# The issuing queue of a fallback path that sits behind a range test: SyncE's hardware queue or GpSimd's software queue

## The chip, the cores and the metric

One core of one Trainium2 chip runs the kernel. The metric is the device time of one execution, in microseconds (us). Engines are named as in the profile: PE (TensorE matmul), PEld (TensorE weight load), DVE (VectorE), ACT (ScalarE), POOL (GpSimd), SP (SyncE). A "q" behind a name (SPq, POOLq) is the engine's sequencer, which issues DMAs, waits on semaphores and branches.

## The reference

Chunked attention feeds a two-layer network with an exact GELU. q, k and v have 8 batches, 8 heads, 576 positions and 64 channels, in f32; a chunk has 64 positions and attends to itself alone.

```
scores = scale * matmul(q_c, k_c.T)          # per chunk of 64
scores = scores - max(scores, axis=-1)
attn   = exp(scores); attn = attn / (sum(attn, axis=-1) + 1e-09)
out    = matmul(attn, v_c)
x = out.transpose(0, 2, 1, 3).reshape(4608, 512)
h = x @ w_in                                  # 512 -> 2048
g = 0.5 * h * (1 + erf(h / sqrt(2)))
return g @ w_out                              # 2048 -> 512, f32
```

## The kernel before, in words

**Fast path.** Everything from line 1093 to line 1331 is written out by hand under a manual schedule, in nine tiles `t` of 512 tokens. Tiles 0 to 7 are the first 512 positions of each batch; tile 8 is the last chunk of all eight batches. For each tile q, k and v are loaded in f32 by SP, cast to bf16 (mostly on POOL), transposed, multiplied, and exponentiated on ACT without taking off the row's maximum. The sums' reciprocals go on DVE. Both matrix products of the network run on PE in 128 x 128 blocks, in tiles from 1 on with seven block products in place of eight (`seven_rows`, `mm2_seven`, lines 598 and 758), GELU on ACT. The results go to DRAM from SP, and in the last tile partly from ACT (`store_block`, line 870; `last_piece`, line 977, whose copy out of PSUM is line 974).

**Range test.** The fast path has not subtracted the maximum, so all its sums of exponentials are kept. `range_test` (line 875) finds per partition whether all lie between 2^-40 and 2^40; `range_count` (line 887) adds the 128 verdicts with a matmul of one column (line 890), and DVE casts the count to an integer (line 891). Then each of the five engines loads that integer into a register (line 1332) and branches on it (line 1333):

```
range_count()
in_range = nc.values_load(total)
with tc.If(in_range < P, preferred_fallthrough_block=False):
    general()
```

With these inputs all 128 partitions are in range, so `general()` isn't entered.

**General path.** `general` (line 893) loads both weights again and casts them, and then runs `one_chunk` (line 910) in two hardware loops over batches and chunks: three loads, attention with the maximum taken off, the network, one store. Its DMAs are issued by SP: lines 899, 904, 915 and 970.

**What the program does at such an If.** Each DMA of the kernel adds 16 to one of eight semaphores of its queue when it has landed, and each engine adds to its own semaphore. So that the counts agree behind the If whichever way it went, the block for the branch not taken into `general` adds what the body would have added once. The profile has this block's instructions under line 1333. Both ways meet in a last block, under line 1358: SP waits for the DMA semaphores, the five sequencers' and the engines' semaphores, then a barrier over five engines, collected and released by POOL, then POOL clears the range of semaphores that was used, then a second barrier. A first barrier of this kind, also collected by POOL, stands at the start, under line 1347, behind a few register moves and four memsets of constants.

Of the kernel before, what the change touches and what calls it, by code (L numbers as in the profile page):

```python
# [11 lines left out]
def kernel(  # L12
# [9 lines left out]
    nc = tc.nc  # L22
# [5 lines left out]
    B, H, S, D = q.shape  # L28
    CH = 64
# [71 lines left out]
    w_in_v = moe_w_in.rearrange("(ks p) n -> p ks n", p=P)  # L101
    w_out_v = moe_w_out.rearrange("(f p) n -> p f n", p=P)
# [15 lines left out]
    def stage_tile():  # L118
        return stage.tile([P, SW], f32, tag="stage", name="arrival")
# [773 lines left out]
    def general():  # L893

        SUBS = mybir.AluOpType.subtract
        for c in range(4):
            n = d_ff // 4
            raw = stage_tile()[:].rearrange("p (ks n) -> p ks n", ks=KS)
            nc.sync.dma_start(raw, w_in_v[:, :, c * n:(c + 1) * n])
            DV(w_in_sb[:, :, c * n:(c + 1) * n], raw)  # L900
        for c in range(4):
            n = FF // 4
            raw = stage_tile()[:].rearrange("p (f n) -> p f n", f=n)
            nc.sync.dma_start(raw, w_out_v[:, c * n:(c + 1) * n, :])
            DV(w_out_sb[:, c * n:(c + 1) * n, :], raw)
        with tc.For_i(0, B, 1) as b:
            with tc.For_i(0, S, CH) as s0:
                one_chunk(b, s0, SUBS)

    def one_chunk(b, s0, SUBS):  # L910
        rows = bass.ds(s0, CH)
        nat = {}
        for nm, src in (("q", q), ("k", k), ("v", v)):
            raw = stage_tile()[0:CH, 0:d_model]
            nc.sync.dma_start(raw.rearrange("p (h d) -> p h d", h=H),
                              src[bass.ds(b, 1), :, rows, :].rearrange("o h key d -> key (o h) d"))
            nat[nm] = ld.tile([P, G, J, 2, D], bf16, tag="k", name=nm + "_rows", bufs=3)[:].rearrange(
                "p g j r d -> p (g j r d)")[0:CH, 0:d_model]
            DV(nat[nm], raw)
        turned = {}  # L920
        for nm in "qk":
            tp = ps_tp.tile([P, G, CH], bf16, tag="tp", name="tp")
            for g in range(G):
                nc.tensor.transpose(tp[:, g], nat[nm][:, P * g:P * (g + 1)], ident[0:CH, 0:CH])
            turned[nm] = work.tile([P, CT, CH], bf16, tag="pT", name=nm + "_t", bufs=5)[:, 0:G]
            DV(turned[nm], tp[:])
        s_ps = [ps_at.tile([P, G, CH], f32, tag="at", name="s_ps") for _ in range(2)]
        top = work.tile([P, 2, 2, NB], f32, tag="total", name="top", bufs=2)[:].rearrange("p a b c -> p (a b c)")
        less = stage_tile()[0:CH, 0:d_model].rearrange("p (g r c) -> p g r c", g=G, r=2)
        for r in range(2):  # L930
            sl = slice(CH * r, CH * (r + 1))
            for g in range(G):
                nc.tensor.matmul(s_ps[r][0:CH, g], turned["q"][sl, g], turned["k"][sl, g], start=True, stop=True)
            m = top[0:CH, G * r:G * (r + 1)]
            nc.vector.tensor_reduce(m, s_ps[r][0:CH], axis=mybir.AxisListType.X, op=mybir.AluOpType.max)
            nc.vector.tensor_tensor(less[:, :, r], s_ps[r][0:CH], m.to_broadcast([CH, G, CH]), op=SUBS)
        less = less.rearrange("p g r c -> p (g r) c")
        e = stage_tile()[0:CH, 0:d_model].rearrange("p (h c) -> p h c", h=H)
        nc.scalar.activation(e, less, Act.Exp, scale=scale)
        nc.vector.tensor_reduce(top[0:CH, H:2 * H], e, axis=mybir.AxisListType.X, op=ADD)  # L940
        nc.vector.tensor_scalar(top[0:CH, H:2 * H], top[0:CH, H:2 * H], 1e-9, None, op0=ADD)
        nc.vector.reciprocal(top[0:CH, 2 * H:3 * H], top[0:CH, H:2 * H])
        a = work.tile([P, CT, CH], bf16, tag="pT", name="a", bufs=5)[0:CH]
        nc.vector.tensor_tensor(a, e, top[0:CH, 2 * H:3 * H].to_broadcast([CH, H, CH]), op=mybir.AluOpType.mult)
        tp = ps_tp.tile([P, H, CH], bf16, tag="tp", name="tp")
        for h in range(H):
            nc.tensor.transpose(tp[0:CH, h], a[:, h], ident[0:CH, 0:CH])
        aT = work.tile([P, CT, CH], bf16, tag="pT", name="a_t", bufs=5)[0:CH]
        DV(aT, tp[0:CH])
        av = ps_at.tile([P, G, CH], f32, tag="at", name="av")  # L950
        for h in range(H):
            sl = slice(CH * (h % 2), CH * (h % 2 + 1))
            nc.tensor.matmul(av[sl, h // 2], nat["v"][:, D * h:D * (h + 1)], aT[:, h], start=True, stop=True)
        x = work.tile([P, CT, CH], bf16, tag="pT", name="x", bufs=5)[:, 0:G]
        DV(x, av[:])
        hb = hpool.tile([P, FF, MT], bf16, tag="h", name="h")[:, :, 0:CH]
        for a0 in range(0, FF, 8):
            h_ps = ps_mm.tile([P, 8, CH], f32, tag="mm", name="h_ps")
            for f in range(8):
                for ks in range(KS):  # L960
                    nc.tensor.matmul(h_ps[:, f], w_in_sb[:, ks, (a0 + f) * P:(a0 + f + 1) * P], x[:, ks],
                                     start=(ks == 0), stop=(ks == KS - 1))
            nc.scalar.activation(hb[:, a0:a0 + 8], h_ps[:], Act.Gelu)
        y_ps = ps_mm.tile([P, d_model], f32, tag="mm", name="y_ps")
        for f in range(FF):
            nc.tensor.matmul(y_ps[0:CH], hb[:, f], w_out_sb[:, f, :], start=(f == 0), stop=(f == FF - 1))
        y_sb = ypool.tile([P, d_model], f32, tag="y", name="y_sb")
        DV(y_sb[0:CH], y_ps[0:CH])
        by_batch = out.rearrange("(b s) d -> b s d", s=S)
        nc.sync.dma_start(by_batch[bass.ds(b, 1), rows].rearrange("o key d -> (o key) d"), y_sb[0:CH])  # L970

    def last_piece(t, m, y_ps):
        y_sb = ypool.tile([P, HD], f32, tag="y", name="y_sb")
# [119 lines left out]
    with tc.manual_schedule():  # L1093
# [62 lines left out]
        for c in range(1, NWC):  # L1156
# [8 lines left out]
            if c < 3:  # L1165
                r = slice(CH * (c - 1), CH * c)
                o = slice(CH * (2 - c), CH * (3 - c))
# [84 lines left out]
        for t in range(1, NT):  # L1252
            n = t + 1
# [79 lines left out]
        with tc.If(in_range < P, preferred_fallthrough_block=False):  # L1333
            general()
# [28 lines left out]
```

## Time and profile before

| what | value |
|---|---|
| median of 3 runs | 267.47 us |
| lowest and highest of them | 267.15 and 268.73 us |
| the profiled execution | 269.52 us |
| its span, first to last instruction | 267.7 us |
| mean granted TensorE clock | 0.993 |
| instructions in the span | 7854 |
| moved by DMA | 54.02 MB, 123415 packets |

The profile is of one execution. Its own time is 269.52 us, 1.8 us more than the span between its first and last instruction, and 2.05 us more than the median of the three runs without a profile. A row of a line's instructions gives the engine, the operation, how many there were, the least, median and greatest duration in ns, and the start of the first and the last in us from the span's start. A row of the timeline has start and duration in us, and in square brackets the idle time before it and what ended it.

### The profile page before, as it was taken

The page shows a single profiled execution, that of the slowest core. Times are in us where ns is not written, and L with a number is a line of the kernel's source. Part 1 is how long each engine was busy: PE and PEld are TensorE (multiplying, and loading weights), DVE is VectorE, ACT ScalarE, POOL GpSimd, SP SyncE. Part 2 cuts the span into 40 slices and gives each one's busy share as a digit, 9 for nine tenths or more (in the row PEclk, how much of TensorE's full clock was granted, in tenths as well). Part 3 has the DMA queues.
Part 4 walks back from the last instruction along what each step waited for, and adds up shares of the span by engine and source line. Part 5 has one row for each costly group of instructions (what it writes and reads, how often), then busy time and mean ns, then how long its engine had stood idle before and what let it go on. Part 6 is the DMA issues. An engine that isn't in the chain of part 4 may idle for free.

```text
span 267.7 us, 7854 instructions
## 1 busy us (share of the span) xinstructions
PE 256.5 (96%) x3116; PEld 211.7 (79%) x3122; DVE 223.3 (83%) x397; ACT 190.4 (71%) x386; POOL 104.7 (39%) x229
## 2 busy tenths in 40 slices
PE   6599999999999999999999999999999999999992
PEld 2378865556888888887888888898888888888881
DVE  5767786998997687678999999999999999848771
ACT  3666667987767978898887588947894788237610
POOL 7778578702375370570390094087211300000000
PEclk9979999999999999999999999999999999999999
DMA  6999998979889999989999998999963310130014
GB/s 198 259 327 399 393 402 213 288 192 284 238 223 247 185 254 254 231 221 249 279 243 207 284 211 219 184 173 210 275 150 86 123 42 2 40 120 1 2 39 122
DMA packets 123415, 54.02 MB, mean 202 GB/s; under 512 B 97776, under 2 KB 120304, under 8 KB 123376
## 3 DMA queue, kind: packets, MB, share of 16 engines
q1 hardware_dynamic: 123072, 53.23, 78.0%
q8 instruction: 25, 0.41, 0.6%
q10 hardware_dynamic: 304, 0.26, 0.3%
q14 instruction: 14, 0.11, 0.1%
HBM read 36.70 MB, written 9.44 MB: 172 GB/s over the span
## 4 chain that ended last, share of the span: by engine, by line
PE 70%; ACT 8%; SPq 7%; DMA 6%; DVE 3%; POOL 2%; issue 2%; POOLq 0%; ACTq 0%
PE hs_ps L598 23%; PE y_ps L758 18%; PE y_ps L788 9%; PE h_ps L462 5%; ACT h L606 3%; DMA arrival<-in_q_dram 3%; SPq L152 3%; SPq L136 3%; PE y_ps L1021 3%; DMA arrival<-in_k_dram 2%; ACT k_bd L219 2%; PE h_ps L478 2%; PE av_ps L346 1%; DMA out_dram<-kept 1%; PE y_ps L985 1%
## 5 line engine op out<-in xcount | busy, mean ns | idle before, releaser
L606 ACT ACTIVATE h<-hs_ps 128x512 bf16<-128x512 f32 x87 | 49.7, 610 | 6.9 <-PE hs_ps L598 6.0
L235 POOL CAST v_nat<-arrival 128x256 bf16<-128x256 f32 x56 | 25.9, 488 | 37.3 <-DMA arrival<-in_v_dram 36.8
L598 PEld LDWEIGHTS <-w_in_sb 128*128 128x128 bf16 x348 | 33.9, 98 | 4.6 <-issue 0.2
L193 POOL CAST q_nat<-arrival 128x256 bf16<-128x256 f32 x40 | 17.9, 495 | 48.3 <-DMA arrival<-in_q_dram 26.8
L598 PE MATMUL hs_ps<-x,w_in_sb 128*128 128x256 bf16 x232 | 31.7, 272 | 0.0
L758 PEld LDWEIGHTS <-h 128*128 128x128 bf16 x240 | 23.2, 98 | 2.8
L1091 ACT ACT_TABLE_LOAD x16 | 20.5, 1283 | 1.0 <-PEq L1347 0.8
L718 ACT COPY kept<-y_ps 128x512 f32<-128x512 f32 (+1 forms) x17 | 9.0, 535 | 16.0 <-PE y_ps L758 13.0
L189 POOL CAST k_nat<-arrival 128x256 bf16<-128x256 f32 x48 | 18.6, 430 | 3.2 <-DMA arrival<-in_k_dram 3.2
L758 PE MATMUL y_ps<-w_out_sb,h 128*128 128x256 bf16 x160 | 18.6, 273 | 0.0
L758 PE MATMUL y_ps<-v_bd,k_bd 128*128 128x256 bf16 x160 | 18.5, 273 | 0.1
L758 PEld LDWEIGHTS <-k_bd 128*128 128x128 bf16 x160 | 15.6, 98 | 2.1 <-issue 0.2
L615 ACT COPY hs_ps<-hs_ps 128x512 f32<-128x512 f32 x29 | 16.2, 582 | 0.6 <-PE hs_ps L598 0.5
L598 PE MATMUL hs_ps<-k_bd,w_in_sb 128*128 128x256 bf16 x116 | 16.6, 273 | 0.0
L490 ACT ACTIVATE h<-h_ps 128x512 bf16<-128x512 f32 x21 | 12.5, 604 | 5.1 <-PE h_ps L462 3.6
L269 ACT ACTIVATE pT<-s_ps 128x512 bf16<-128x512 f32 x28 | 14.4, 599 | 1.8 <-PE s_ps L261 1.8
L788 PEld LDWEIGHTS <-h 128*128 128x128 bf16 x144 | 13.8, 98 | 1.7
L598 PE MATMUL hs_ps<-k_bd,w_in_more 128*128 128x256 bf16 x96 | 14.2, 273 | 0.0
L462 PE MATMUL h_ps<-x,w_in_sb 128*128 128x256 bf16 x128 | 14.2, 273 | 0.0
L598 PEld LDWEIGHTS <-w_in_more 128*128 128x128 bf16 x128 | 12.5, 98 | 2.0 <-issue 0.3
L723 DVE TENSOR_TENSOR kept<-y_ps,kept 128x512 f32<-128x512 f32 (+1 forms) x16 | 10.4, 651 | 4.0 <-PE y_ps L758 2.3
L462 PEld LDWEIGHTS <-w_in_sb 128*128 128x128 bf16 x128 | 12.4, 98 | 1.6 <-DVE w_in_sb L1066 0.2
(174 smaller groups left out, 640.2 us busy)
## 6 DMA issues: line engine op xcount, KB each, us to landing
arrival<-in_v_dram SPq DMA_DIRECT2D x58, 128.0 KB, 3.2
arrival<-in_k_dram SPq DMA_DIRECT2D x28, 256.0 KB, 5.8
arrival<-in_q_dram SPq DMA_DIRECT2D x7, 1024.0 KB, 6.7
out_dram<-kept SPq DMA_DIRECT2D x24, 256.0 KB, 3.1
arrival<-in_moe_w_out_dram SPq DMA_DIRECT2D x4, 1024.0 KB, 12.4
arrival<-in_moe_w_in_dram SPq DMA_DIRECT2D x6, 512.0 KB, 7.9
out_dram<-y_sb SPq DMA_DIRECT2D x8, 256.0 KB, 3.1
arrival<-in_v_dram SPq DMA_DIRECT2D x28, 64.0 KB, 2.8
```

Of the source, the lines that this page charges most:

```text
L189: copy(st[nm][:, q0:q0 + 2, g], st[nm + "f"][:, 2 * q0:2 * q0 + 4, g].rearrange("p (q r) d -> p q r d", r=2))
L193: copy(st[nm][:, g, j:j + 2].rearrange("p j r d -> p r j d"), st[nm + "f"][:, 2 * g:2 * g + 2, j:j + 2])
L235: copy(st["v"][:, r::2, n], st["vf"][:, r::2, n])
L269: nc.scalar.activation(pT[:].rearrange("p u (c j) -> p u c j", j=J), tiles[t]["s_ps"][m // 2][m % 2][:].rearrange("p u (j c) -> p u c j", ...
L462: nc.tensor.matmul(to[:, cols], left, right[:, cols], start=(start and a == 0), stop=stop, skip_group_check=True)
L490: nc.scalar.activation(tiles[t]["h"][:, f, :], h_ps[:], Act.Gelu)
L598: nc.tensor.matmul(hs[:, f], left[:, ks, f * P:(f + 1) * P], right[:, ks], start=(fresh and f == 0 and ks == 0), stop=(ks == 1), skip_grou ...
L606: nc.scalar.activation(h[:, n:n + HM, HD * c:HD * (c + 1)], src, Act.Gelu)
L615: "s11": lambda: AC(place_of("b")[:], bank["a"][:]),
L758: nc.tensor.matmul(to, left(f, m), right[:, f], start=(fresh and (split or m == 0) and f == 0), stop=(f == HF - 1), skip_group_check=True)
L788: nc.tensor.matmul(bank[name][:, m], left(f, m), right[:, f], start=(fresh and m == 0 and f == 0), stop=(f == HF - 1), skip_group_check=True)
L1091: nc.scalar.activation(act_scratch[:], rest[:, 0:1], func)
```

## The change

All DMAs of the general path are issued by GpSimd (POOL) on its software queue, where they were issued by SP on its hardware queue: four loads of `w_in`, four of `w_out`, and per chunk the loads of q, k and v and the store.

```
@@ general
-            nc.sync.dma_start(raw, w_in_v[:, :, c * n:(c + 1) * n])
+            nc.gpsimd.dma_start(raw, w_in_v[:, :, c * n:(c + 1) * n])
...
-            nc.sync.dma_start(raw, w_out_v[:, c * n:(c + 1) * n, :])
+            nc.gpsimd.dma_start(raw, w_out_v[:, c * n:(c + 1) * n, :])
@@ one_chunk
-            nc.sync.dma_start(raw.rearrange("p (h d) -> p h d", h=H),
+            nc.gpsimd.dma_start(raw.rearrange("p (h d) -> p h d", h=H),
...
-        nc.sync.dma_start(by_batch[bass.ds(b, 1), rows].rearrange("o key d -> (o key) d"), y_sb[0:CH])
+        nc.gpsimd.dma_start(by_batch[bass.ds(b, 1), rows].rearrange("o key d -> (o key) d"), y_sb[0:CH])
```

In the built programs the 7,742 instructions between the first barrier and the branch are the same on every engine, but that ACT once counts two instructions one by one where it added 2 behind the second. Outside `general` these differ:

| place | before | after |
|---|---|---|
| start, line 1347 | SP: 4 register moves ahead of the barrier | POOL: the 4 register moves, behind its INC_SWDGE_SEM and ahead of its memsets |
| not-taken block, line 1333, SP | 8 EVENT_SEMAPHORE, each waits for one of the 8 DMA semaphores of SP's queue and adds to it; branch | branch alone |
| not-taken block, POOL | branch alone | 4 EVENT_SEMAPHORE on the 8 new semaphores of the software queue (waits for 0 or more), one INC_SWDGE_SEM that adds 16 or 32 to each of the 8, branch |
| last block, line 1358, SP | 8 EVENT_SEMAPHORE, the last for ACT's last store | 4 more ahead of these, each waits for two of the new semaphores to have what INC_SWDGE_SEM adds |
| last block, POOL | clears 17 semaphores | clears 25 |
| instructions that the branch to the last block jumps over | SP 91, POOL 44 (ACT 51, DVE 70) | SP 62, POOL 91 (ACT 59, DVE 79) |

INC_SWDGE_SEM is in the program before once, at its start, with no semaphore to add to.

## The prediction

> **What bounds the kernel now.** I read the page first: engine shares, then the chain that ended last.
>
> ```profile
> span 267.7 us, 7854 instructions
> ...
> PE 256.5 (96%) x3116; PEld 211.7 (79%) x3122; DVE 223.3 (83%) x397; ACT 190.4 (71%) x386; POOL 104.7 (39%) x229
> ...
> PE 70%; ACT 8%; SPq 7%; DMA 6%; DVE 3%; POOL 2%; issue 2%; POOLq 0%; ACTq 0%
> ```
>
> PE is busy for 96% of the span and carries 70% of the chain. The diff touches nothing that PE does before the branch, so the question is what lies outside that stretch. The table by windows cuts the span into start, body, last matmuls and tail, and the chain from 250 us on shows where the last compute ends.
>
> ```profile
> 0.00:10.00 10.00, 6.46 (x40) 2.62 (x40) 5.88 (x12) 4.31 (x7) 7.00 (x25) 1.00 0.83 242
> 10.00:239.00 229.00, 226.47 (x2862) 188.19 (x2869) 199.49 (x351) 173.65 (x356) 97.66 (x205) 0.99 0.87 219
> 239.00:262.50 23.50, 23.50 (x217) 20.88 (x214) 17.42 (x33) 12.42 (x25) 0.00 (x0) 1.00 0.13 35
> 262.50:267.70 5.20, 0.10 (x2) 0.01 (x1) 0.48 (x2) 0.00 (x0) 0.00 (x0) 0.96 0.38 107
> ```
> ```profile
> 250.28 12.24 PE y_ps L758 x112
> 262.52 0.02 issue
> 262.54 0.43 DVE y_sb L974
> 262.97 0.05 DVE small L891
> ```
>
> The columns of the windows are busy PE, PEld, DVE, ACT, POOL, then clock, DMA share and GB/s. In the last 5.2 us no engine computes more than 0.48 us: that tail consists of stores landing and of sequencers. There, and at the first barrier, lies all that the change can move. Next I read the instructions of each line of the tail.
>
> ```profile
> L977 SPq DMA_DIRECT2D out_dram<-y_sb x2: 490/492/494, 262.1 to 263.0; - x2
> ...
> DMA to landing us min/median/max: 2.0/2.2/2.4
> ```
> ```profile
> L1332 POOLq TENSOR_LOAD <-small x1: 489/489/489, 263.1 to 263.1; - x1
> ...
> L1332 SPq TENSOR_LOAD <-small x1: 953/953/953, 263.5 to 263.5; - x1
> ```
> ```profile
> L1333 SPq EVENT_SEMAPHORE  x8: 17/17/17, 265.0 to 265.5; - x8
> L1333 POOLq COMPARE_BRANCH  x2: 38/42/45, 263.6 to 263.7; - x2
> ...
> L1333 DVEq COMPARE_BRANCH  x2: 51/53/55, 263.8 to 264.0; - x2
> L1333 SPq COMPARE_BRANCH  x2: 38/48/57, 264.6 to 265.5; - x2
> L1333 ACTq COMPARE_BRANCH  x2: 38/44/49, 264.6 to 264.8; - x2
> ```
> ```profile
> L1358 SPq EVENT_SEMAPHORE  x8: 28/28/28, 266.1 to 266.5; - x8
> L1358 SPq DRAIN  x2: 7/10/13, 266.6 to 266.6; - x2
> L1358 POOLq DRAIN  x1: 41/41/41, 263.8 to 263.8; - x1
> ...
> L1358 DVEq DRAIN  x1: 47/47/47, 264.6 to 264.6; - x1
> L1358 ACTq DRAIN  x1: 8/8/8, 264.9 to 264.9; - x1
> L1358 POOLq EVENT_SEMAPHORE  x1: 17/17/17, 266.7 to 266.7; - x1
> ```
>
> Only SP is late. POOL, DVE and ACT stand at their DRAIN of the last block by 263.8, 264.6 and 264.9; SP reaches its own at 266.6 and POOL's barrier starts at 266.7. SP's way there: the last store is issued at 263.0 (0.49 us), the register is loaded from 263.5 (0.95), the branch comes at 264.6, the first of the eight additions of the not-taken block runs at 265.0 (the store of 263.0, at the least 2.0 us to landing, ends that wait), the eighth at 265.5, so 0.5/7 = 0.07 us each. The second branch at 265.5 reaches the last block at 266.1, and its eight waits take until 266.5: 0.4/7 = 0.06 us each.
>
> **The change, part by part.** `general` isn't entered, so none of its loads and stores is run, and no transfer moves from one queue to another in this execution. What is run and differs is four pieces of sequencer work.
>
> 1. SP's eight additions go. SP then meets its two branches as POOL does now, 0.1 us apart: the second at 264.7 in place of 265.5. The landing that held the first addition until 265.0 is next asked for in the last block.
>
> 2. SP's jump. The rows give two sizes: POOL 263.7 to 263.8 and ACT 264.8 to 264.9, 0.1 us; DVE 264.0 to 264.6 and SP 265.5 to 266.1, 0.6. ACT skips 51 instructions and DVE 70; SP will skip 62, between them, so 0.1 and 0.6 are the ends, and I take 0.5, near SP's own row: it reaches the last block at 265.2 (264.8 to 265.3).
>
> 3. SP's last block has twelve waits in place of eight: 12 x 0.06 = 0.75 us, to 265.95. The hardware queue's landings cannot hold it: SP's and ACT's last stores are issued at 263.0 and land 2.0 to 2.4 us later, at 265.4 at the latest, and the wait for ACT's is the twelfth. Before, this point was 266.55. So pieces 1 to 3 give -0.6 us, with ends of -1.0 and -0.5.
>
> 4. POOL's additions. Four waits that hold at once, and one INC_SWDGE_SEM that adds to eight semaphores. The trace has this operation once, with nothing to add, at the start:
>
> ```profile
> L1347 POOLq EVENT_SEMAPHORE  x2: 17/17/17, 0.6 to 0.6; - x2
> L1347 POOLq INC_SWDGE_SEM  x1: 27/27/27, 0.1 to 0.1; - x1
> L1347 POOL MEMSET const-float32-0.0<- x1: 104/104/104, 0.2 to 0.2; 128x1 f32 x1
> ...
> L1347 POOLq DRAIN  x1: 197/197/197, 0.3 to 0.3; - x1
> ```
> ```profile
> L1347 SPq MOVE  x4: 29/34/42, 0.0 to 0.2; - x4
> L1347 SPq DRAIN  x1: 7/7/7, 0.3 to 0.3; - x1
> ```
> ```profile
> L1358 POOLq EVENT_SEMAPHORE_RANGE_CLEAR  x1: 135/135/135, 267.3 to 267.3; - x1
> ```
>
> POOL branches at 263.7; four waits at no more than 0.1 us each put INC_SWDGE_SEM at 264.1 at the latest. Call its time until all eight semaphores are seen x. SP asks for them from 265.2 on, so x up to 1.1 us costs nothing: the cover is SP's longer register load and its jump, and beyond it every us of x is a us of the end. POOL's own jump now skips 91 instructions as SP's did, 0.6 us, and ends at 264.8 + x, also before 265.95. From the rows x is at the least the 0.03 us of the empty form. Eight additions one after the other at SP's rate are 8 x 0.07 = 0.55; a clear of 17 semaphores in one operation took 0.135. The far end is a landing, 2.4 us, if the additions travel as those of a DMA do. I take 0.5, by the nearest row, SP's additions of the same amounts: hidden.
>
> 5. The clear of 25 semaphores in place of 17 lies on the path: between nothing and 0.135 x 8/17 = +0.06; I take +0.05.
>
> 6. The start. POOL runs four moves that SP ran, ahead of its memsets and its DRAIN; the other engines are at the barrier by 0.3 and POOL collects it at 0.6, so POOL is last and the moves delay all that follows. At 0.034 us of duration they cost 0.14; at SP's pitch (four in 0.3 us) 0.3. I take +0.2. SP's loss of the moves brings nothing, as it waits for POOL.
>
> Sum: -0.6 + 0 + 0.05 + 0.2 = -0.35 us. The profiled execution took 269.52 us, 1.8 more than its span; so 269.15. The median of the runs shown, 267.47, is 2.05 lower, and becomes 267.1.
>
> [...] The page's instruction-fetch queue reads:
>
> ```profile
> q8 instruction: 25, 0.41, 0.6%
> ...
> q14 instruction: 14, 0.11, 0.1%
> ```
>
> By the first row a fetch is 0.6% of 16 engines' 267.7 us over 25 packets, about 1.0 us. [...]
>
> **The rivals.**
>
> A. Slower: the additions land as a DMA's do. x is then 2.0 to 2.4 us, SP sees the semaphores at 266.1 to 266.5 in place of 265.2, and +0.9 to +1.3 comes on top: 268.0 to 268.4. It decides from x = 1.1 + 0.35 = 1.45 us on. For it: these semaphores belong to the software queue, and all that the trace shows of DMA semaphores are landings. Against it: the empty form took 0.03 us, and a memset followed it from 0.2 on.
>
> B. Slower by much: POOL must bring in the code of an operation that it has run only in its empty form. The nearest row of such a load is ACT's:
>
> ```profile
> L1091 ACT ACT_TABLE_LOAD x1 | 1.3, 1283 | 0.8 <-PEq L1347 0.8
> ```
>
> At 1.3 us, beside the 0.5 of the additions, x is 1.8: +0.7 on the sum, 267.8. Two or more such loads in a row reach 269 to 271. [...] The trace has nothing of the kind in the one use it shows.
>
> C. Nothing changes: the not-taken way is not bound by SP's additions, for instance because SP's jump takes as long as it needs for the block to be there, whenever it is asked. SP's last block would then start at 266.0 still (-0.1), four more waits come on top (+0.25), and pieces 5 and 6 add 0.25: +0.4, 267.9 at the most; with half of that loss, 267.7. That the change does nothing at all to the executed instructions is excluded by the list of the two programs.
>
> **How the numbers follow.** The forecast, a small gain of 0.1 to 0.8 us (266.7 to 267.4), has 0.55. Rival A has 0.2, B 0.12 (a third of it within 1%), C 0.13. A per cent is 2.7 us, about what a measurement of this kernel can tell from no change. The range must hold the forecast, A and C, and the spread of the median itself (the three runs before lie from 267.15 to 268.73): 266.3 to 268.7. Beyond 1%: faster 0.01, since all SP's sequencer time between 264.6 and 266.5 is less than 2.7 us; slower 0.08, the far part of B. The rest, 0.91, is within 1%.
>
> **What would show it.** SP's rows under line 1333: two COMPARE_BRANCH about 0.1 us apart and no EVENT_SEMAPHORE; under line 1358 twelve waits, the first about 2.7 us behind the start of the last copy (265.2 less 262.54). A first wait much later, with POOL's INC_SWDGE_SEM long or its semaphores late, is A or B. A first wait at 266 with POOL done by 265 is C. At the start POOL's barrier at 0.75 in place of 0.6. A body that differs, between 10 and 262 us, would make the whole account wrong, as would a longer time outside the span: 1.8 us here, which holds nothing that I can cost.

## The result and the profile after

The kernel after takes 267.37 us (median of 22 runs, 266.05 to 268.92), the kernel before in the same session 268.25 us (22 runs, 267.15 to 270.15). The ratio is 0.9964 with a 95% interval of 0.9948 to 0.998, so the change is worth -0.96 us (-1.4 to -0.5). Ratios here leave out disturbed runs, which the medians beside them contain, so the two need not agree to the last digit.

The forecast was -0.35 us, to 267.1 us. The change is within 1%, a small gain as forecast, and the time lies in the range; but the gain is larger than the sum said, and 0.96 us lies above the 0.1 to 0.8 us of the forecast, though the interval reaches into them. That 267.37 us comes so near to 267.1 is luck: the forecast started from a median of three runs, 267.47 us, which lay 0.78 us below the 268.25 of all 22. The profiled execution of the kernel after took 266.46 us.

First its page and its table by windows, in the columns of the one shown for before: PE, PEld, DVE, ACT, POOL busy, clock, DMA share, GB/s.

```profile
span 264.9 us, 7861 instructions
...
PE 255.6 (97%) x3122; PEld 210.7 (80%) x3122; DVE 223.4 (84%) x397; ACT 190.6 (72%) x386; POOL 106.7 (40%) x229
```
```profile
10.00:239.00 229.00, 227.29 (x2885) 188.72 (x2883) 200.27 (x353) 174.99 (x357) 99.36 (x204) 1.00 0.88 221
239.00:260.60 21.60, 21.60 (x199) 19.17 (x197) 16.56 (x32) 11.19 (x23) 0.00 (x0) 1.00 0.11 26
260.60:264.90 4.30, 0.07 (x1) 0.00 (x0) 0.47 (x2) 0.00 (x0) 0.00 (x0) 0.93 0.46 131
```

The spans differ by 2.8 us, three times what the runs show. Most of that lies ahead of the last copy, in work that is the same in both programs: the copy starts at 262.54 us before and at 260.62 here. In second profiles of the same two kernels it starts at 260.39 and 261.37, the other way about. A single pair of spans cannot show a change of 1 us in this kernel. What repeats is the tail, from the start of the last copy (line 974) to the end: 5.19 and 5.17 us before, 4.30 and 4.29 after. All times "behind the copy" below count from there and are taken from the records in ns; the rows give the same to 0.1 us.

The rows of the not-taken block, of the last block and of the last copy in the kernel after:

```profile
260.62 0.42 DVE L974 COPY y_sb<-y_ps 128x256 f32<-128x256 f32 x1 [0.45 <-PE y_ps L758]
```
```profile
L1333 POOLq EVENT_SEMAPHORE  x4: 17/43/43, 261.9 to 262.1; - x4
L1333 POOLq COMPARE_BRANCH  x2: 38/42/45, 261.8 to 262.4; - x2
...
L1333 SPq COMPARE_BRANCH  x2: 38/50/61, 262.6 to 262.8; - x2
...
L1333 POOLq INC_SWDGE_SEM  x1: 173/173/173, 262.2 to 262.2; - x1
```
```profile
L1358 SPq EVENT_SEMAPHORE  x14: 17/28/28, 263.3 to 264.9; - x14
L1358 POOLq EVENT_SEMAPHORE  x4: 17/17/17, 264.1 to 264.8; - x4
...
L1358 SPq DRAIN  x3: 7/7/13, 264.0 to 264.4; - x3
...
L1358 POOLq EVENT_SEMAPHORE_RANGE_CLEAR  x1: 178/178/178, 264.4 to 264.4; - x1
```

SP has no additions under line 1333, and its two branches stand 0.11 us apart. Its second branch comes 2.14 us behind the copy (before: 3.00), its twelve waits start at 2.65 (before: eight, at 3.51), and it reaches its DRAIN at 3.42 (before: 4.03). That is -0.61 us. POOL's four waits and its INC_SWDGE_SEM of 0.17 us are over by 1.75, long before SP asks for them.

The rest of the tail is POOL's closing barrier. These are its first two semaphore instructions there, in narrow windows of the two traces, before and then after:

```profile
L1358 POOLq EVENT_SEMAPHORE  x2: 17/17/17, 266.7 to 267.0; - x2
```
```profile
L1358 POOLq EVENT_SEMAPHORE  x2: 17/17/17, 264.1 to 264.2; - x2
```

Before, 0.37 us lie between their starts, after 0.09: -0.28 us, at a place where the diff changes nothing. The clear of the semaphores took 0.178 us in place of 0.135 (+0.04), the DRAIN ahead of it 0.09 in place of 0.15. SP's -0.61, the pause's -0.28 and the clear's +0.04 with the DRAIN's -0.06 add up to -0.91, where the tail lost 0.89.

The start did move as forecast, from before to after:

```profile
0.25 0.10 POOL L1347 MEMSET const-float32-0.0<- 128x1 f32 x1 [0.25 <-issue]
...
4.50 0.40 PE L206 MATMUL tp<-ident,q_nat 128*128 128x128 bf16 x4
```
```profile
0.48 0.10 POOL L1347 MEMSET const-float32-0.0<- 128x1 f32 x1 [0.48 <-issue]
...
4.73 0.46 PE L206 MATMUL tp<-ident,q_nat 128*128 128x128 bf16 x4
```

POOL's first memset and the first matmul on data are both 0.23 us later behind the first instruction of the span. Yet the measured time doesn't carry it: time less span is 1.8 us before and 1.58 after (medians over all runs), 0.22 less. The section on the reasons comes back to this.

### The profile page after: what moved, and what is told of

Its sections match the earlier page's. It is cut to its first block, busy times and chain, and to the rows that moved or that the text cites. A ratio compares the mean times of both kernels' runs of the same rounds, so it can differ in the third digit from the quotient of the medians.

```text
span 264.9 us, 7861 instructions
## 1 busy us (share of the span) xinstructions
PE 255.6 (97%) x3122; PEld 210.7 (80%) x3122; DVE 223.4 (84%) x397; ACT 190.6 (72%) x386; POOL 106.7 (40%) x229
## 4 chain that ended last, share of the span: by engine, by line
PE 84%; ACT 8%; DVE 3%; DMA 2%; issue 1%; SPq 1%; POOL 0%; POOLq 0%
PE hs_ps L598 29%; PE y_ps L758 22%; PE y_ps L788 12%; PE h_ps L462 5%; PE y_ps L1021 3%; ACT h L606 3%; PE h_ps L488 2%; DMA arrival<-in_k_dram 2%; ACT k_bd L219 2%; PE av_ps L346 2%; PE h_ps L478 2%; ACT pT L269 2%; PE y_ps L985 1%; PE s_ps L261 1%; PE y_ps L462 1%
## 5 line engine op out<-in xcount | busy, mean ns | idle before, releaser
L189 POOL CAST k_nat<-arrival 128x256 bf16<-128x256 f32 x48 | 20.1, 467 | 2.6 <-DMA arrival<-in_k_dram 2.6
```

The lines of the kernel that those rows point to most:

```text
L189: copy(st[nm][:, q0:q0 + 2, g], st[nm + "f"][:, 2 * q0:2 * q0 + 4, g].rearrange("p (q r) d -> p q r d", r=2))
```

## The experiments

Twelve kernels were run. The table gives what the tail of each shows, in us behind the start of its last copy; "pause" is the time between the starts of POOL's first two semaphore instructions in the closing barrier, "position" the place of POOL's last block in its program, counted in instructions of the built program.

| kernel | SP's second branch | SP's DRAIN | pause | position | tail | tail less 5.19 | ratio to before, 95% interval |
|---|---|---|---|---|---|---|---|
| before, twice | 3.00, 2.98 | 4.03, 4.00 | 0.37, 0.37 | 324 | 5.19, 5.17 | 0 | 1 |
| after, twice | 2.14, 2.13 | 3.42, 3.42 | 0.09, 0.09 | 380 | 4.30, 4.29 | -0.89 | 0.9964 (0.9948 to 0.998) |
| chunk | 2.99 | 4.14 | 0.09 | 361 | 5.02 | -0.17 | 1.0015 (0.9987 to 1.0042) |
| weights | 2.43 | 3.70 | 0.09 | 351 | 4.58 | -0.61 | 0.9955 (0.9918 to 0.9992) |
| act | 2.99 | 4.03 | 0.37 | 324 | 5.19 | 0.00 | 0.9972 (0.994 to 1.0004) |
| empty | 2.14 | 2.96 | 0.08 | 281 | 3.76 | -1.43 | 0.9937 (0.9909 to 0.9965) |
| place | 2.11 | 2.94 | 0.09 | 324 | 3.75 | -1.44 | 0.9964 (0.9932 to 0.9996) |
| pad | 3.00 | 4.03 | 0.08 | 372 | 4.83 | -0.36 | one run |
| page | 2.99 | 4.01 | 0.37 | 452 | 5.17 | -0.02 | one run |
| early9 | 1.10 | 4.21 | 0.09 | 380 | 5.09 | -0.10 | 1.0023 (0.9997 to 1.0049) |
| early9_sp | 4.43 | 5.45 | 0.37 | 324 | 6.61 | +1.42 | 1.0057 (1.0034 to 1.008) |
| early_two | 1.10 | 2.90 | 0.09 | 380 | 3.78 | -1.41 | 0.9939 (0.9907 to 0.9972) |

At some 268 us, all measured intervals but one hold what the tail says; early9's misses it by a hair (-0.08 to +1.3 us for a tail of -0.10). The intervals are 0.4 to 1 us to either side, though, so that by times alone after (0.9964) and act (0.9972) are not told apart. The causes below rest on the tails.

**The two kernels again.** No edit.

> The kernel before once more, for a second trace. Theory 1 (the gain is sequencer work behind the last copy): from the start of the last copy of line 974 to the end of the span 5.2 us as in the first trace (267.7 less 262.5), with POOL's 0.4 us between its two semaphore instructions of the first closing barrier (266.7 and 267.0). Rival (the two traces differ by chance): the tail comes out anywhere between 4.3 and 5.2, or the 0.4 is not there again.

> The changed kernel once more. Theory 1: the tail is 4.3 us again (264.9 less 260.6), SP's first wait of the last block 2.65 us behind the start of the last copy, INC_SWDGE_SEM 0.17 us, time less span 1.55 us. Rival (chance): the tail is between 4.3 and 5.2 us, and time less span anywhere up to 1.8.

They took 267.34 and 267.2 us, one run each, with tails of 5.17 and 4.29. Every step of the tail repeats within 0.03 us; the place of the last copy does not, within 2 us.

**One part of the change alone.** In `chunk` only the four DMAs of `one_chunk` go to GpSimd, in `weights` only the eight weight loads.

```
@@ chunk: one_chunk
-            nc.sync.dma_start(raw.rearrange("p (h d) -> p h d", h=H),
+            nc.gpsimd.dma_start(raw.rearrange("p (h d) -> p h d", h=H),
...
-        nc.sync.dma_start(by_batch[bass.ds(b, 1), rows].rearrange("o key d -> (o key) d"), y_sb[0:CH])
+        nc.gpsimd.dma_start(by_batch[bass.ds(b, 1), rows].rearrange("o key d -> (o key) d"), y_sb[0:CH])
@@ weights: general
-            nc.sync.dma_start(raw, w_in_v[:, :, c * n:(c + 1) * n])
+            nc.gpsimd.dma_start(raw, w_in_v[:, :, c * n:(c + 1) * n])
...
-            nc.sync.dma_start(raw, w_out_v[:, c * n:(c + 1) * n, :])
+            nc.gpsimd.dma_start(raw, w_out_v[:, c * n:(c + 1) * n, :])
```

> Only the four transfers of a chunk go to the software queue, the weights stay on SP. SP keeps its 8 additions, the last block has 10 waits, POOL has the 4 moves at the start and 4 semaphores to add to. Theory 1 with 'the start is not in the metric': tail 5.2 + 2 x 0.06 - 0.3 (POOL's gap gone, as its last block lies elsewhere in its program) = 5.0 us, POOL's first barrier 0.23 us later but time less span 1.55, so time -0.1 to -0.2 us against before. Rival 'the start counts', the prediction's piece 6: time less span 1.8 and +0.05 to +0.1 us. Rival 'the software queue itself brings the gain': as the whole change, about -0.9 us.

> Only the eight loads of the weights go to the software queue. SP keeps 4 additions and the 4 moves at the start; the last block has 12 waits, POOL adds to 8 semaphores. Theory 1: 4 x 0.07 fewer for SP, 4 x 0.06 more, POOL's gap gone (-0.3), clear +0.04: tail 4.9 us, time less span 1.8, time -0.2 to -0.3 us. Rival 'the software queue itself brings the gain': tail 4.3 us, time -0.9 us. Rival 'the start counts': nothing to count here, the start as before, so the same -0.2 to -0.3 and no help in telling it apart but by time less span, which it leaves at 1.8 in both parts.

SP's rows of the not-taken block, of chunk and then of weights (last copies at 260.46 and 260.57):

```profile
L1333 SPq EVENT_SEMAPHORE  x8: 17/17/17, 262.9 to 263.4; - x8
L1333 SPq COMPARE_BRANCH  x2: 38/48/57, 262.5 to 263.4; - x2
```
```profile
L1333 SPq EVENT_SEMAPHORE  x4: 17/17/17, 262.7 to 262.9; - x4
L1333 SPq COMPARE_BRANCH  x2: 38/48/57, 262.6 to 263.0; - x2
```

Chunk keeps all eight additions, and SP is as late as before. So a GpSimd queue in the general path does not itself shorten SP's way; what counts is how many additions SP is left with, and on which semaphores. Its tail is 0.17 us shorter all the same, because the pause is gone, while SP's two more waits cost 0.12. Weights went further than expected (4.58 for 4.9): its four additions, as many as there are DMAs of `one_chunk` on SP, are on semaphores other than that of SP's last store, so they start at 2.14 and not at the landing of 2.42. The additions thus cost in two ways here: 0.07 us each, and the wait for a landing under the first of them, 0.3 us.

**Another hardware queue.** All DMAs of the general path on ScalarE.

```
-            nc.sync.dma_start(raw, w_in_v[:, :, c * n:(c + 1) * n])
+            nc.scalar.dma_start(raw, w_in_v[:, :, c * n:(c + 1) * n])
...
```

> The transfers of the general path are issued on ScalarE's hardware queue. Theory: what counts is not that SyncE's queue is free of them but that no hardware queue needs additions with waits for landings in the block not taken; SyncE still adds to eight semaphores for ACT's queue or ScalarE does, GpSimd's last block stays at 324 with its pause of 0.37, the tail stays at 5.1 to 5.3 us, and the time is that of the kernel before within 0.3% (ratio 1.000). Rival (it is enough to free SyncE, which is the last to the closing barrier by 1.7 us; ScalarE is early): the tail falls to 4.4 to 4.6, and the ratio is 0.997 to 0.998.

SP's row of the not-taken block (last copy at 261.57):

```profile
L1333 SPq EVENT_SEMAPHORE  x8: 17/17/17, 264.0 to 264.5; - x8
```

SP still runs the eight additions, each step of the tail is that of before within 0.02 us, and the pause is there. It is not enough that the general path leaves SP's queue. The semaphore numbers in the trace records fit this: in before, SP's 206 DMAs add to all eight semaphores and ACT's three stores to three of the same eight (the records have 16 landings for a DMA: 432 for the 27 DMAs on the semaphore of SP's last store). So they are not the semaphores of SP's queue alone, as the description of the kernel before has it, but serve both hardware queues, and SP makes the additions for both. The ratio's interval just holds 1.

**Without the general path.** `empty` leaves the general path out, with one memset in its place, so it cannot compute what that path is for.

```
-            general()
+            nc.vector.memset(act_scratch[:], 0.0)
```

> The general path is left out: behind the test stands one memset on DVE, so a run whose sums were out of range would not be mended; the fast path is whole. No DMA semaphore is added to by any engine and no software queue is used. Theory 1 (SP's additions and the jump over general set the end): SP's two branches 0.1 us apart, a jump over 2 instructions 0.1 us, first wait of the last block 2.3 us behind the start of the last copy, held by the landings to 2.4 and 2.7, eight waits to 2.85, then 0.85 to 0.9 to the end: tail 3.75 us, time -1.4 us against before. Rival (what counts is that POOL's queue takes the transfers): no software queue, so the tail stays at 5.2 and the time as before.

As expected: 3.76. SP's jump is over two instructions, and it stands at its last block when its last store lands. Against this floor, the kernel after still pays 0.54 us for having the general path: SP's jump (0.51 in place of 0.29, at whose end the landing stands), four waits (0.25) and the longer clear (0.04) are 0.51 of it.

**The pause.** Three kernels move POOL's last block by memsets that do nothing. `pad` puts 48 on a new tile into the kernel before, `place` 43 into empty (it too leaves the general path out), `page` 128 into the kernel before.

```
@@ page (place: 43, in the kernel empty; pad: 48 on a new tile idle)
+        for _ in range(128):
+            nc.gpsimd.memset(act_scratch[:], 0.0)
         range_count()
```

> The kernel before with 48 memsets of one column more on POOL ahead of the range count, when POOL is idle; they move what follows by 48 places in POOL's program and change nothing else. It tells what the 0.37 us is that POOL takes between its two semaphore instructions in the first closing barrier of the kernel before, 0.09 after. Theory 'a fixed boundary in POOL's program lies in the last block': the gap is 0.09 and the tail 4.9 us. Rival 'the distance from the jump counts: what lies 46 or more places behind POOL's branch isn't at hand yet': the distance is the same 44, so the gap is 0.37 again and the tail 5.2. Second rival (chance): neither.

> The kernel empty (the general path left out, one VectorE memset in its place) with 43 memsets of one column on GpSimd ahead of the late count, so that GpSimd's last block stands at instruction 324 of its program, where it stands in the kernel before, and not at 281. Theory (GpSimd's pause of 0.37 us in place of 0.09 between two semaphore instructions of its first closing barrier belongs to a place in the program): the pause is 0.37 again and the tail 4.0 to 4.05 us in place of 3.76. Rival (the pause needs the skipped instructions of the general path, or the jump over 44 of them): 0.08 and a tail of 3.76. If the 48 memsets of the kernel pad were what made its body some 8 us longer, this kernel's body is some 7 us longer too; if the added tile in pad was it, it is not.

> The kernel before with 128 memsets of one column on GpSimd ahead of the late count, all on a tile that exists already. GpSimd's last block then stands at instruction 452 of its program, 128 behind its place in the kernel before, and its jump is still over 44 instructions. The pause of 0.37 us came with a last block at 324 behind a jump over 44 (before, act, early9_sp), and not at 372 behind the same jump (pad), nor at 324 without a jump over general's code (place). [...] Rival (it belongs to that one place, or to something else that these kernels share): 0.08 to 0.09, and a tail of 4.83 as in pad. [...]

POOL's rows of page, in a narrow window as above:

```profile
L1360 POOLq EVENT_SEMAPHORE  x2: 17/17/17, 265.2 to 265.6; - x2
```

With the same jump over 44 instructions, the pause is gone at position 372 and back at 452, 128 behind 324. At 324 with nothing to jump over (place) it is not there: the theory that I had put down for that run fell, since position alone doesn't make the pause. With the jump it came back 128 instructions on, with 0.37 and a tail of 5.17, where the rival of page had 0.08 to 0.09 and 4.83. That fits a period of 128, but two places with the pause and one without leave 64 and 32 open too. The small instruction fetches bring 8 KB each (q14 of before: 14, 0.11 MB). By an estimate from the trace of before, where all fetches bring 0.52 MB for 7854 instructions (66 bytes each), that is some 124 instructions, about the step of 128 that was tried. That the pause is such a fetch is not shown, and the records rather speak against it. The pause begins 4.13 us behind the copy in before. A fetch of about 0.5 us does start 4.04 to 4.07 us behind the copy in before and act, but in chunk too, which has no pause; and page, which has the pause, has its fetch at 4.34, as pad has, which has none. The records do not say which engine a small fetch is for.

Pad took 275.82 us in its one run; its last copy comes 7 to 9 us later than in the two traces of before, a lag that builds up between 70 and 200 us. Page has more memsets and took 268.07, so the memsets aren't why; whether the added tile was, or that one run, is open.

**SP's way taken off the path.** In `early9` the count is taken in slot 9 of the last tile, and SP and ACT load their registers ahead of their last stores. `early9_sp` is the same edit in the kernel before.

```
+    def early_count():
+        range_count()
+        for engine in (E.SP, E.Activation):
+            nc.reg_load(regs[engine], total)
...
+                e2.setdefault(9, []).append(early_count)
...
-        range_count()
-        in_range = nc.values_load(total)
+        for engine in (E.PE, E.DVE, E.Pool):
+            nc.reg_load(regs[engine], total)
+        in_range = nc.snap(regs, donate=True)
```

> The changed kernel, with the range count four matmul groups earlier and the register load of SP and ACT right behind it, ahead of their last stores (PE, DVE and POOL load at the end as before). Theory 1 (behind the last copy SP's register load of 0.95 us is the next thing on the path, and behind that the landing of the last store): SP branches 1.0 us behind the copy's start in place of 2.0, its first four waits are done by 1.9, the hardware queues' landings hold it at 2.4 and 2.7, drain at 2.9: tail 3.8 us against 4.3. PE may lose 0.2 us for the earlier count: time -0.3 us against the changed kernel, -1.2 against before. Rival (the register load is not on the path): tail 4.3, time no better than the changed kernel or 0.2 worse.

> The same earlier load in the kernel before, so with SP's eight additions. Theory 1: the first addition asks for the landing of SP's last store (2.4 us behind the copy's start), so SP's earlier branch only waits there; eight additions, jump, eight waits follow as before: tail 5.2 us, time within 0.2 us of before. Rival (the register load is what SP's lateness comes from): tail 4.2 us, time -1 us against before.

SP branched early, as it should, but both missed: the last stores landed late. The landings of the last stores, and the DMA queues between 1.3 and 2.0 us behind the copy, in early9 (q8 is taken to be the queue of PE's instructions: before, it brings 0.41 of 0.52 MB, 79%, and PE and PEld have 6,238 of the 7,854 instructions, 79%):

```profile
DMA to landing us min/median/max: 2.4/3.3/3.4
```
```profile
q1 hardware_dynamic: 73, 0.06, 32.8%
q10 hardware_dynamic: 79, 0.07, 32.0%
q8 instruction: 1, 0.02, 10.1%
```

In the kernels before and after, PE loads its register behind the cast of the count, and a fetch on its queue starts at 2.5 to 3.0, 1.0 to 1.5 us behind its branch (empty and place, which have nothing of the general path to jump over, lack this fetch). In early9 it doesn't wait for the cast, branches at 0.15, and 16 KB are fetched from 1.54 on, for 1.1 us, while the last stores are under way. Of each store one 4-byte packet is late (at 3.11 and 3.35; the others at 1.8 to 2.3), and with it the landing: 3.70 and 3.86 in place of 2.40 and 2.68. SP in its last block waits for it, and the tail is 5.09. In early9_sp PE's fetch ends at 2.81 in place of 2.68, and the two late packets are 0.13 later as well (3.24 and 3.48): in both kernels they start 0.43 and 0.67 us behind the end of the fetch. There SP's first addition waits for the landing at 3.84, and the tail is 6.61.

**The same with PE left late.** `early_two` takes the count twice: early into a second cell for SP and ACT, late for PE, DVE and POOL as in the kernel after.

```
@@ early_two, against early9
+        range_count(soon)
         for engine in (E.SP, E.Activation):
-            nc.reg_load(regs[engine], total)
+            nc.reg_load(regs[engine], soon)
...
+        range_count(total)
         for engine in (E.PE, E.DVE, E.Pool):
             nc.reg_load(regs[engine], total)
```

> The kernel after, but SyncE and ScalarE get the count early: a matmul of one column and a cast in the 9th slot of the last tile put it into a second cell, from which these two load their registers ahead of their last stores; the late count stays as it was for TensorE, VectorE and GpSimd. Theory (what held the last stores back in early9 was TensorE's own instruction fetch of 16 KB, which started at 1.54 us behind the last copy's start since TensorE no longer waited for the late cast): TensorE's load waits for the cast again, its fetch starts at 2.5 to 2.6, the last stores land at 2.4 and 2.7 as in the kernel after, and the tail falls from 4.30 to about 3.8 us, 0.5 below the kernel after and some 1.4 below the kernel before (ratio near 0.995). Rival (the early branches of SyncE and ScalarE themselves bring the landings to 3.7 to 3.9, by their own fetches): the landings stay there, the tail at 5.1, and the ratio at 1.002 as in early9.

Landings, SP's branches and the last block of early_two, whose last copy is at 264.54, with the fetches from 2.4 us behind it on:

```profile
DMA to landing us min/median/max: 1.9/2.3/2.4
```
```profile
L1345 SPq COMPARE_BRANCH  x2: 38/50/61, 265.5 to 265.6; - x2
```
```profile
L1370 SPq EVENT_SEMAPHORE  x14: 17/28/28, 266.2 to 268.3; - x14
...
L1370 SPq DRAIN  x3: 7/7/13, 267.4 to 267.8; - x3
```
```profile
q8 instruction: 1, 0.02, 6.2%
q14 instruction: 2, 0.02, 3.9%
```

With PE's fetch back at 2.55 the stores land at 2.40 and 2.73, and the tail is 3.78, as expected. SP branches 1.0 us behind the copy as in early9, and the small fetches (q14) from 2.3 on do no harm; so the rival falls. POOL, which loaded its register early in early9, is late again here too, but the fixed distances above tie the late packets to PE's fetch. By its tail this is the fastest kernel here that computes all, 0.5 us below the kernel after; by its time, 0.9939 (0.9907 to 0.9972) of before, it is not told apart from that one. It stops at the landing of SP's last store: the fifth wait of the last block is held until 2.41.

## Why the prediction was right in sign and short in size

- **Pieces 1 to 3 (SP's additions, its jump, its waits): -0.6 forecast, -0.61 measured.** Each point fits: second branch at 264.7 - 262.54 = 2.16 (2.14), last block at 2.66 (2.65), end of the waits at 3.41 (3.42). The jump over 62 instructions took 0.51, as SP's over 91 did before, where the rounded rows gave 0.6. (12 x 0.06 is 0.72, and not the 0.75 of the sum; the twelve waits took 0.77.) The runs add what the working left unsaid: the additions hold for a landing, and weights, which frees SP of that, gains 0.3 us by it.
- **Piece 4 (POOL's additions, hidden): right.** INC_SWDGE_SEM took 0.17 us. SP found its four waits met at 2.65, so x is at most 1.1 and rival A (2.0 and more) is out; no code load shows ahead of it or in it, so rival B is out, with the far part that the 0.08 for slower stood on.
- **The jumps.** They agree with the rows of before, and are shorter than a fetch of PE's instructions (0.88 to 1.49 us in before): from the start of the branch SP's jump is 0.51 us, POOL's over 91 instructions 0.44, before over 44 0.16. PE's fetch moves with PE's branch: in early9 PE branches at 0.15 and the fetch starts at 1.54 us behind the copy, in early_two, where PE's load waits for the late cast again, at 2.55. The pause came only with a jump over general's code (page and place), but that it is a fetch is not shown, nor that any jump waited for one.
- **Piece 5 (the clear): +0.05 forecast, +0.04 measured.**
- **Piece 6 (the start): this is the step that failed.** "POOL is last and the moves delay all that follows": they do, by 0.23 us for the 0.2 forecast, but the time does not carry them. In all but one of the 14 profiles, time is the last semaphore write less POOL's first memset, plus 0.12 us (0.115 to 0.122; early9: 0.20). The four moves stand ahead of that memset. The prediction took the 1.8 us outside the span as a constant and named "a longer time outside the span" as a danger; it became shorter instead, by just the 0.22 us of the moves. So this term is 0, and the sum -0.55.
- **A term that was missing: POOL's pause, -0.28.** The list of the two programs had POOL's jump at 44 and 91 instructions, and the rows for before had 0.3 us between POOL's barrier instructions at 266.7 and 267.0, but no piece asked why. The code that the change adds ahead of POOL's last block moves it from 324 to 380 and makes its jump longer; pad, with the jump of before, shows that a move off that place is enough. Why the pause comes there stays open. This part of the gain is an accident of the code's length; no queue has to do with it.
- **Rival C: out.** SP's last block came 0.86 us earlier (2.65 for 3.51), not at the old time, and SP's jump took 0.51 us in both kernels.

With the two corrections and the shorter DRAIN, -0.61 - 0.28 + 0.04 - 0.06 = -0.91 us, inside the measured -1.4 to -0.5. The forecast's own sum, -0.35, lies outside it.

## What to carry to other kernels

The general path that was not entered still cost what keeps the counts right: with the hardware queues one semaphore instruction on SP, also where ACT issues (act), for each semaphore that the DMAs behind the branch add to (eight in before, four in weights; 0.07 us each, and 0.3 us for the landing of a late store); with the software queue four waits and one instruction of 0.17 us on an engine that was early, and four more waits on SP in the last block (0.25 us). It pays to ask which engine is last at the closing barrier, and to load its branch register ahead of its last store (0.5 us here), while the engine with the large fetch stays behind the stores (early_two's tail of 3.78 us against early9's 5.09). For changes under 1 us compare the stage that they touch from an event that both kernels share, since the body moved the last copy by 2 us between profiles of one kernel.

## What the runs showed of the hardware

- The time behaves as if it began with POOL's first memset, and not with the register moves ahead of it: time less span is 1.80 us in before, where these stand on SP, 1.82 in weights, where they also do, and 1.58 (after), 1.54 (chunk), 1.60 (early_two) where they stand on POOL. A start at anything that keeps its distance from that memset would do as well, such as POOL's collection of the first barrier, 0.31 us behind it before and after.
- POOL paused 0.37 in place of 0.09 us between two semaphore instructions whenever its last block stood at 324 or 452 behind a jump over 44 instructions (before, act, early9_sp, page), and not in the kernels tried with another place or another jump.
- A fetch of PE's instructions, 16 KB in 1.1 us, held one packet of each of two stores that were under way and moved their landings from 2.4 and 2.7 to 3.7 and 3.9 us behind the copy (early9). Why these two packets waited is not shown: the records do not name the DMA engines.
- Act's time less span is 1.95 us (median of 12 runs; before in the same session 1.83), though in its profile POOL's first memset starts at 0.24 us, as before. This stayed open.
